# Moving four transpose pairs within the gate matmuls of an S5-plus-SwiGLU kernel with one PSUM slot for them

## The chip, the cores and the metric

The kernel runs on one core of one Trainium2 chip. The metric is the device time of one execution in microseconds (us), the median over several runs. A profile of one execution of each kernel goes with it. PE is the engine of the matmuls, PEld its weight loads, DVE is VectorE, ACT is ScalarE, POOL is GpSimd, and SP issues most DMAs. The later runs were made on three chips (numbers 0, 2 and 9 in the record), so times are compared only with those of before in the same rounds on the same chip, unless the text says otherwise.

## The reference, cut to what matters

```python
x  = A_x                                  # 1 x 2048 x 512, bfloat16
xn = layernorm(x)
return x + S5(xn, Lambda, B, C, dt, Dskip) \
         + (silu(xn @ w_gate) * (xn @ w_up)) @ w_down      # 512 -> 1376 -> 512
```

S5 is a diagonal complex recurrence over the 2048 tokens, between two matrix products of 512 x 512. All matmuls want `xn` with features on the partitions, so `xn` has to be transposed. The change touches only the first 512 tokens (four tiles of 128). Their transposes run on PE, through PSUM. The other tokens are transposed by DMA.

## The kernel before: the parts that matter

The kernel is written as a graph of tasks. PE and SP run their tasks in the order of the program. The orders of the other engines come from a list scheduler that works with estimated times. Semaphore waits are derived from what each task reads and writes. A task that reads or writes PSUM names whole banks:

```python
def BK(b):
    return [("bk", b, 0), ("bk", b, 1)]
...
for t in stream:                      # emission of one engine's stream
    for sem, val in t.waits:
        eng_obj.wait_ge(sem, val)     # t.waits: list of a dict that was filled
    inst = t.fn(eng_obj)              # in the order of a Python set
```

The first stage computes seven of the gate's column tiles for the first 512 tokens. It goes by quarters `q` of 128 tokens, so that it can start when the first tile of `x` is normalised. Seven of the eight PSUM banks accumulate these seven tiles. One bank is left, and all transposes of tiles 1 to 3 go through it (`xt_pair[0]`, here called the slot). A tile's 512 features are transposed in two halves of two 128x128 transposes each. After each half an engine copies the slot to SBUF.

```python
def xt_tile_fine(a, h, slot=None):            # tile a, half h
    slot = xt_pair[0] if slot is None else slot
    def tr2(e):
        for j in range(2):
            inst = e.transpose(out=ptr[:, slot, j*128:(j+1)*128], in_=xn_sb[...], identity=ident[:])   # cut; L582
        return inst
    g.add("pe", tr2, reads=[("xh", a, h), ("ident",)], writes=BK(slot), ...)
    if a == 3:     # VectorE copies the half, L589
    elif h == 0:   # ScalarE copies it in two pieces of 128 columns, L592
    else:          # ScalarE copies it in one piece of 256 columns, L597
...
place = {(0, 2, 4): (1, 0), (1, 0, 3): (1, 1), (1, 2, 2): (2, 0), (2, 0, 4): (2, 1), (2, 2, 2): (3, 0), (3, 0, 2): (3, 1)}
for q in range(4):
    for k0, k1 in (((0,1),(1,2),(2,3),(3,4)), ((0,1),(1,2),(2,4)), ((0,1),(1,2),(2,4)), ((0,2),(2,4)))[q]:
        for n, (i, bk) in enumerate(tiles):           # seven gate tiles
            if (q, k0, n) in place:
                xt_tile_fine(*place[(q, k0, n)])
            # matmuls kt = k0 .. k1-1 of gate tile i, tokens of quarter q          (L803)
            # reads xnT of tile q, features kt
ffn_mm(0, NQ, "g", xt_pair[0])       # the eighth gate tile, whole: 128x512 matmuls, L759
```

A quarter is 28 matmuls of 128x128. `place` says in front of which of them a transpose pair stands. So the second half of tile 1 (`(1, 1)`) has three things to wait for: VectorE's normalised operand, ScalarE's copy of the first half out of the slot, and PE's own order. The matmuls of quarter 1 with `kt` 2 and 3 then wait for the copy of that second half.

Of the kernel before, what the change touches and what calls it, by code (L numbers as in the profile page):

```python
# [249 lines left out]
def bass_parallel_sum__ssm_conv_s5__swiglu_ffn__prompt_kernel(  # L250
# [32 lines left out]
    with es:  # L283
# [87 lines left out]
        def next_pair():  # L371
            for _ in range(NB // 2):
                b = 2 * (pair_ctr[0] % (NB // 2))
                pair_ctr[0] += 1
                if not (b in reserved or _bank_live(b) or _bank_live(b + 1)):
                    return b
            raise AssertionError("all PSUM pairs live")
# [4 lines left out]
        def BK(b):  # L382
            return [("bk", b, 0), ("bk", b, 1)]
# [81 lines left out]
        def act_table(func, order):  # L465
            g.add("act", lambda e: e.activation(out=sm[:, NSM - 1, 0:1], in_=epst[:], func=func, bias=epst[:, 0:1]), reads=[("epst",)], writes=[("sm", "_warm")],
                  name="act_warm", est=1500, order=order)
# [3 lines left out]
        def pe_warm(n, w=512, bk=None):  # L471
            if bk is None:
                bk = next_pair()

            def mm(e, bk=bk):
                for _ in range(n):
                    inst = e.matmul(pbank[:, bk, 0:w], lhsT=one.to_broadcast([128, 128]), rhs=one.to_broadcast([128, w]), start=True, stop=True)
                return inst
            g.add("pe", mm, writes=BK(bk), name="pe_warm", est=n * w * 0.84, ninst=n)
# [96 lines left out]
        def xt_tile_fine(a, h, slot=None):  # L576
# [4 lines that stand above are left out]
                    kt = h * 2 + j  # L581
                    inst = e.transpose(out=ptr[:, slot, j * 128:(j + 1) * 128],  # L582
                                       in_=xn_sb[:, a % NXN, kt * 128:(kt + 1) * 128], identity=ident[:])
                return inst
            g.add("pe", tr2, reads=[("xh", a, h), ("ident",)], writes=BK(slot), name="xT%d_%d" % (a, h), est=2 * 64, ninst=2)
            dst, src = xnT[:, 0, a % 4, 2 * h:2 * h + 2, :], ptr[:, slot, 0:256].rearrange("p (k t) -> p k t", k=2)
            wr = [("xnTq", a, 2 * h + j) for j in range(2)] + ([("xnT", 0, a % 4)] if h else [])
            if a == 3:
                t = g.add("dve", lambda e: e.tensor_copy(out=dst, in_=src), reads=BK(slot), writes=wr, name="xTev%d_%d" % (a, h), est=320, order=(hold["xn3"],))  # L589
            elif h == 0:  # L590
                for j in range(2):
                    t = g.add("act", lambda e, j=j: e.activation(out=dst[:, j], in_=src[:, j], func=AF.Identity), reads=BK(slot), writes=wr[j:j + 1],  # L592
                              name="xTev%d_0%d" % (a, j), est=240, order=(t,) if j else ())
                    if j == 0:
                        hold["ev%da" % a] = t
            else:
                t = g.add("act", lambda e: e.activation(out=dst, in_=src, func=AF.Identity), reads=BK(slot), writes=wr, name="xTev%d_%d" % (a, h), est=340)  # L597
            hold["ev%d%d" % (a, h)] = t
# [154 lines left out]
        def ffn_mm(c, i, which, bk):  # L753
            fs = fsz[i]
            w = wg if which == "g" else wu

            def mm(e, bk=bk, w=w, i=i, fs=fs, c=c):
                for kt in range(KT):
                    inst = e.matmul(pbank[0:fs, bk, :].rearrange("p (j t) -> p j t", j=4), lhsT=w[:, kt, i * 128:i * 128 + fs], rhs=xnT[:, c % 2, :, kt, :],  # L759
                                    start=(kt == 0), stop=(kt == KT - 1))  # L760
                return inst
            g.add("pe", mm, reads=wres("wg" if which == "g" else "wu", i) + [("xnT", c % 2, j) for j in range(4)],
                  writes=BK(bk), name="mm_%s%d_%d" % (which, c, i), est=4 * 216, ninst=4)

        def silu_pair(c, ip, bk):
            i0, n = FP[ip]
            rows = slice(0, 128)
            sl = gctr[0] % NG
            gctr[0] += 1
            sg_slot[(c, ip)] = sl  # L770
            g.add("act", lambda e: e.activation(out=sg[rows, sl, 0:n, :].rearrange("p a t -> p (a t)"), in_=pair_f32(rows, bk, 512 * n), func=AF.Silu),  # L771
                  reads=sum([BK(bk + k) for k in range(n)], []), writes=[("sg", sl)], name="silu%d_%d" % (c, ip), est=63 + 427 * n)
# [8 lines left out]
        def ffn_gate_quarters(pairs):  # L781
            banks = {ip: next_pair() for ip in pairs}
            reserved.update(banks.values())
            tiles = [(2 * ip + k, banks[ip] + k) for ip in pairs for k in range(2)]
            xt_pair[0] = tiles.pop()[1]
            wbank = tiles[-1][1]
            pe_warm(9, 512, wbank)
            pe_warm(2, 128, wbank)
            ln_chunk0()
            xt_tile_fine(0, 0, wbank)  # L790
            pe_warm(1, 256, tiles[-2][1])
            xt_tile_fine(0, 1)
            pe_warm(1, 256, tiles[-2][1])
            place = {(0, 2, 4): (1, 0), (1, 0, 3): (1, 1), (1, 2, 2): (2, 0), (2, 0, 4): (2, 1), (2, 2, 2): (3, 0), (3, 0, 2): (3, 1)}
            for q in range(4):
                for k0, k1 in (((0, 1), (1, 2), (2, 3), (3, 4)), ((0, 1), (1, 2), (2, 4)), ((0, 1), (1, 2), (2, 4)), ((0, 2), (2, 4)))[q]:
                    for n, (i, bk) in enumerate(tiles):
                        if (q, k0, n) in place:
                            xt_tile_fine(*place[(q, k0, n)])

                        def mm(e, bk=bk, i=i, q=q, k0=k0, k1=k1):
                            for kt in range(k0, k1):
                                inst = e.matmul(pbank[:, bk, q * 128:(q + 1) * 128], lhsT=wg[:, kt, i * 128:(i + 1) * 128], rhs=xnT[:, 0, q, kt, :],  # L803
                                                start=(kt == 0), stop=(kt == KT - 1))
                            return inst
                        g.add("pe", mm, reads=[("wg", "a%d" % max(k - 1, 0)) for k in range(k0, k1)] + [("xnTq", q, k) for k in range(k0, k1)], writes=BK(bk),
                              name="mm_gq%d_%d_%d" % (i, q, k0), est=(k1 - k0) * 56, ninst=k1 - k0)
            reserved.clear()
            seq = ["sd0", "negm0", "nmr0", "xa01", "ev0a", "ev00", "sd1", "ev01", "ev1a", "ev10", "sd2", "ev11", "ev2a", "ev20", "sd3", "ev21"]
            for a_, b_ in zip(seq, seq[1:]):  # L810
                hold[b_].od.add(hold[a_])
            act_table(AF.Silu, (hold["ev21"],))
            hold["evac"] = g.tasks[-1]
            ffn_mm(0, NQ, "g", xt_pair[0])
            for ip in pairs:
                silu_pair(0, ip, banks[ip])
            hold["evac"] = [t for t in g.tasks if t.name == "silu0_0"][0]
# [124 lines left out]
        def dc_chunk(c, mid=None, split_last=False):  # L942
# [22 lines left out]
            for (lt, c0, nc_), bk in zip(items, banks):  # L965
# [13 lines left out]
                if nc_ == 128 and c0 == 256:  # L979
# [3 lines left out]
                    reads=[("xo", a, c) for c in ((256, 384) if nc_ == 128 else (c0,))], out_=True)  # L983

        ffn_gate_quarters([0, 1, 2, 3])
        params_a()
        tables()
# [103 lines left out]
```

## Time and profile before

| | before |
|---|---|
| time, first three runs | 179.34 us median (179.16 to 179.64) |
| span of the profiled run | 177.4 us |
| PE busy, VectorE busy | 98%, 92% |
| gate stage (first 128x128 gate matmul to first 128x512 one) | 5.770 to 12.826 us: 7.056 us |
| steps between matmuls over 56 ns in that stage | 134 ns in sum |

Part 1 and part 4 of the page of before: each engine's busy time with its share of the span, and the chain of work that ended last.

```profile
PE 173.6 (98%) x927; PEld 83.8 (47%) x935; DVE 162.5 (92%) x284; ACT 88.1 (50%) x116; POOL 9.0 (5%) x22
...
PE 95%; DMA 1%; DVE 1%; ACT 1%; issue 0%
```

The list of what PE waited for, in before (engine, line, releaser: total us, times, longest):

```profile
PE pb L477 <- PEq L1076: 0.8, 1, 0.8
PE pb L582 <- ACT xn_sb L548: 0.2, 1, 0.2
```

Both waits lie ahead of the gate stage. PE is nearly the whole chain. So the time is the start-up, plus PE's own work, plus whatever PE waits in the gate stage. The list does not show those last waits: they are tens of nanoseconds long and hidden in the overlap of pipelined matmuls. One has to look at starts. PE's timeline of before (start us, us, engine, line, operation, count), with L582 a transpose pair and L803 the gate matmuls between:

```profile
6.77 0.28 PE L582 MATMUL pb<-ident,xn_sb 128*128 128x128 bf16 x2
6.88 0.89 PE L803 MATMUL pb<-xnT,wg 128*128 128x128 bf16 x13
7.61 0.28 PE L582 MATMUL pb<-ident,xn_sb 128*128 128x128 bf16 x2
7.72 1.04 PE L803 MATMUL pb<-xnT,wg 128*128 128x128 bf16 x15
8.60 0.28 PE L582 MATMUL pb<-ident,xn_sb 128*128 128x128 bf16 x2
8.71 0.94 PE L803 MATMUL pb<-xnT,wg 128*128 128x128 bf16 x14
9.50 0.27 PE L582 MATMUL pb<-ident,xn_sb 128*128 128x128 bf16 x2
9.61 1.03 PE L803 MATMUL pb<-xnT,wg 128*128 128x128 bf16 x14
10.48 0.28 PE L582 MATMUL pb<-ident,xn_sb 128*128 128x128 bf16 x2
...
12.83 0.38 PE L759 MATMUL pb<-xnT,wg 128*128 128x512 bf16 x1
```

Read it as start to next start over the count. The 13 matmuls from 6.88 to 7.61 take 0.73 us, 56 ns each, so nothing waits there. The 15 from 7.72 to 8.60 take 0.88 us where 15 x 56 ns are 0.84, so about 40 ns are lost. The 14 from 9.61 to 10.48 take 0.87 us where 0.78 are due, so about 90 ns are lost. The single matmuls of the trace give the exact steps: 25 + 11 ns extra at 8.36 us, 8 ns at 9.50, 80 + 10 ns at 10.25. In this document "excess" is the sum of what such steps take over 56 ns.

Why PE waits at 8.36 and 10.25 us, and why the second transposes stand where they stand, is in ScalarE's timeline and in that of the weight loads, both of before. L592 copies a first half, L597 a second half:

```profile
7.08 0.45 ACT L592 ACTIVATE xnT<-pb 128x128 bf16<-128x128 bf16 x2 [0.70 <-PE pb L582]
...
7.92 0.38 ACT L597 ACTIVATE xnT<-pb 128x256 bf16<-128x256 bf16 x1
8.91 0.45 ACT L592 ACTIVATE xnT<-pb 128x128 bf16<-128x128 bf16 x2 [0.60 <-PE pb L582]
```

```profile
7.58 0.13 PEld L582 LDWEIGHTS pb<-ident,xn_sb 128*128 128x128 bf16 x2
...
9.47 0.13 PEld L582 LDWEIGHTS pb<-ident,xn_sb 128*128 128x128 bf16 x2
```

The copy of tile 1's first half ends at 7.53 us, and the weight load of its second transpose starts at 7.58. The copy of tile 2's first half ends at 9.35 us (8.91 + 0.45, to 0.01), and the weight load of its second transpose starts at 9.47.

### The profile page before, as it was taken

Reading aid. Unit: us, or ns where it says so; the run is one execution under the profiler, and the core shown is the slowest. Engines: PE = TensorE matmul, PEld = TensorE weight load, DVE = VectorE, ACT = ScalarE, POOL = GpSimd, SP = SyncE. Lnnn points to the kernel's source line nnn. Section 1 sums busy time; section 2 is a strip of 40 time slices with the busy share of each in tenths; the row PEclk is TensorE's granted clock in tenths of the full one; section 3 lists DMA queues with packets and bytes.
Section 4 is the critical chain, followed back from the end, with each engine's and each line's share of the span. In section 5 each row is a group of like instructions: output and inputs, shape, how many; then the busy total and the mean of one; then the engine's idle time right before and its main releaser. Section 6 shows DMA issues by size and latency. Waiting matters only on the chain.

```text
span 177.4 us, 2421 instructions
## 1 busy us (share of the span) xinstructions
PE 173.6 (98%) x927; PEld 83.8 (47%) x935; DVE 162.5 (92%) x284; ACT 88.1 (50%) x116; POOL 9.0 (5%) x22
## 2 busy tenths in 40 slices
PE   8999999999999999999999999999999999999994
PEld 2894444444444444444444444444444444444743
DVE  2956999799999999999999999999899999999933
ACT  4679989689999665044565560000965520000000
POOL 3023200040000000300000000000000000000000
PEclk9999999999999999999999999999999999999999
DMA  5994662664951000002600000002000000001022
GB/s 165 315 371 115 139 124 59 163 136 115 351 107 20 0 0 0 0 30 77 133 3 0 0 0 4 0 30 83 5 0 4 0 0 0 0 0 52 11 89 89
DMA packets 23014, 12.37 MB, mean 70 GB/s; under 512 B 15228, under 2 KB 23004, under 8 KB 23004
## 3 DMA queue, kind: packets, MB, share of 16 engines
q1 hardware_dynamic: 22508, 11.54, 23.9%
q10 hardware_dynamic: 496, 0.69, 1.1%
q8 instruction: 7, 0.11, 0.2%
q14 instruction: 3, 0.02, 0.0%
HBM read 6.46 MB, written 2.10 MB: 48 GB/s over the span
## 4 chain that ended last, share of the span: by engine, by line
PE 95%; DMA 1%; DVE 1%; ACT 1%; issue 0%
PE pb L759 36%; PE pb L959 21%; PE pb L876 16%; PE pb L972 15%; PE pb L803 4%; PE pb L839 2%; DMA x_sb<-in_A_x_dram 1%; PE pb L849 1%; PE pb L582 1%; DVE st L530 0%; ACT xn_sb L548 0%; ACT nm L545 0%; ACT sd L524 0%; DVE x_sb L977 0%; DVE mv L522 0%
## 5 line engine op out<-in xcount | busy, mean ns | idle before, releaser
L916 DVE TENSOR_TENSOR_SCAN rot<-sm,car,rot 128x512 bf16<-128x512 f32 x32 | 38.9, 1266 | 0.1
L959 PE MATMUL pb<-wd,hT 128*128 128x512 bf16 (+3 forms) x194 | 38.1, 355 | 0.2
L759 PE MATMUL pb<-xnT,wu 128*128 128x512 bf16 x160 | 37.3, 379 | 0.0
L759 PE MATMUL pb<-xnT,wg 128*128 128x512 bf16 x132 | 31.3, 379 | 0.0
L972 PE MATMUL pb<-W,hss 128*128 128x512 bf16 (+2 forms) x140 | 28.1, 355 | 0.2
L876 PE MATMUL pb<-xnT,BT 128*128 128x512 bf16 x128 | 28.1, 379 | 0.0
L959 PEld LDWEIGHTS pb<-wd,hT 128*128 128x128 bf16 (+1 forms) x198 | 18.5, 98 | 19.9
L759 PEld LDWEIGHTS pb<-xnT,wu 128*128 128x128 bf16 x160 | 15.6, 98 | 18.9 <-issue 0.2
L771 ACT ACTIVATE sg<-pb 128x1024 bf16<-128x1024 f32 x20 | 20.2, 1025 | 8.6 <-PE pb L759 7.8
L829 ACT ACTIVATE uf<-pb 128x1024 bf16<-128x1024 f32 x20 | 20.6, 1029 | 7.2 <-PE pb L759 6.1
L972 PEld LDWEIGHTS pb<-W,hss 128*128 128x128 bf16 x144 | 13.5, 98 | 14.3
L759 PEld LDWEIGHTS pb<-xnT,wg 128*128 128x128 bf16 x132 | 12.7, 98 | 15.7 <-issue 0.4
L876 PEld LDWEIGHTS pb<-xnT,BT 128*128 128x128 bf16 x128 | 12.5, 98 | 15.1
L883 ACT ACTIVATE u_sb<-pb 128x1024 bf16<-128x1024 f32 x16 | 16.2, 1018 | 5.6 <-PE pb L876 5.4
L977 DVE TENSOR_TENSOR x_sb<-pb,x_sb 128x512 bf16<-128x512 f32 (+2 forms) x18 | 11.0, 622 | 3.5 <-PE pb L972 3.4
L831 DVE TENSOR_TENSOR hT<-sg,uf 128x1024 bf16<-128x1024 bf16 x20 | 13.3, 679 | 0.0
L506 ACT ACTIVATE xn_sb<-x_sb,nmr,rstd 128x512 bf16<-128x512 bf16 x8 | 6.0, 803 | 9.2 <-DVE nmr L503 9.2
L858 ACT ACTIVATE sg<-pb 96x1024 bf16<-96x1024 f32 x2 | 2.0, 1014 | 17.1 <-PE pb L839 17.1
L482 DVE BATCH_NORM_STATS2 st<-x_sb 128x6 f32<-128x512 bf16 x12 | 7.4, 678 | 2.9 <-DMA x_sb<-in_A_x_dram 2.9
L907 DVE TENSOR_TENSOR rot<-rot,cosT 128x2048 bf16<-128x2048 bf16 x8 | 9.7, 1216 | 0.1
L907 DVE TENSOR_TENSOR rot<-rot,sin 128x2048 bf16<-128x2048 bf16 x8 | 9.7, 1217 | 0.0
L907 DVE TENSOR_TENSOR rot<-u_sb,cosT 128x2048 bf16<-128x2048 bf16 x8 | 9.7, 1215 | 0.0
(81 smaller groups left out, 143.3 us busy)
## 6 DMA issues: line engine op xcount, KB each, us to landing
out_dram<-x_sb SPq DMA_DIRECT2D x15, 128.0 KB, 1.7
x_sb<-in_A_x_dram SPq DMA_DIRECT2D x3, 512.0 KB, 7.0
wd<-in_B_w_down_dram SPq DMA_DIRECT2D x1, 1280.0 KB, 6.4
wu<-in_B_w_up_dram SPq DMA_DIRECT2D x1, 768.0 KB, 5.1
wu<-in_B_w_up_dram SPq DMA_DIRECT2D x1, 608.0 KB, 7.2
x_sb<-in_A_x_dram SPq DMA_DIRECT2D x4, 128.0 KB, 3.3
wg<-in_B_w_gate_dram SPq DMA_DIRECT2D x1, 480.0 KB, 6.0
wg<-in_B_w_gate_dram ACTq DMA_DIRECT2D x1, 448.0 KB, 3.8
```

What stands on the lines that cost most here:

```text
L482: return g.add("dve", lambda e, a=a: e.bn_stats(out=st[:, a, :], in_=x_sb[:, a, :]), reads=[("x", a)], writes=[("st", a)], name="bnst%d" % ...
L759: inst = e.matmul(pbank[0:fs, bk, :].rearrange("p (j t) -> p j t", j=4), lhsT=w[:, kt, i * 128:i * 128 + fs], rhs=xnT[:, c % 2, :, kt, :], ...
L771: g.add("act", lambda e: e.activation(out=sg[rows, sl, 0:n, :].rearrange("p a t -> p (a t)"), in_=pair_f32(rows, bk, 512 * n), func=AF.Sil ...
L829: g.add("act", lambda e: e.activation(out=uf[rows, ul, 0:n, :].rearrange("p a t -> p (a t)"), in_=pair_f32(rows, bk, 512 * n), func=AF.Ide ...
L831: g.add("dve", lambda e: e.tensor_tensor(out=hT[rows, hb, i0:i0 + n, :], in0=sg[rows, sl, 0:n, :], in1=uf[rows, ul, 0:n, :], op=ALU.mult), ...
L876: inst = e.matmul(pbank[:, bk, :].rearrange("p (j t) -> p j t", j=4), lhsT=BT[:, ri, kt, pt * 128:(pt + 1) * 128], rhs=xnT[:, c % 2, :, kt ...
L883: g.add("act", lambda e: e.activation(out=u_sb[:, us].rearrange("p r t -> p (r t)"), in_=pair_f32(slice(0, 128), b0), func=AF.Identity), r ...
L907: tt = lambda out, a, b, op, r, w, nm: g.add("dve", lambda e: e.tensor_tensor(out=out, in0=a, in1=b, op=op), reads=r, writes=w, name="%s_% ...
L916: g.add("dve", lambda e, A0=A0, A1=A1, k=k, ri=ri, pt=pt: e.tensor_tensor_scan(out=A1[:, k, ri, :], data0=rr[:, pt:pt + 1].to_broadcast([1 ...
L959: inst = e.matmul(pbank[:, bk, 0:nc_], lhsT=hT[0:fs, hb, i, lt * 128:(lt + 1) * 128], rhs=wd[0:fs, i, c0:c0 + nc_], start=(i == 0), stop=F ...
L972: inst = e.matmul(pbank[:, bk, 0:nc_], lhsT=hss[:, hb, pt, ri, lt * 128:(lt + 1) * 128], rhs=W12[:, ri, pt, c0:c0 + nc_], start=False, sto ...
L977: g.add("dve", lambda e, bk=bk, a=a, c0=c0, nc_=nc_: e.tensor_tensor(out=x_sb[:, a, c0:c0 + nc_], in0=pbank[:, bk, 0:nc_], in1=x_sb[:, a, ...
```

## The change

The intent is plain from the excess at 8.36 and 10.25 us. The transposes whose results come late go sooner in PE's order: tile 1's second half by one gate matmul, tile 2's second half by two, both halves of tile 3 by one place of two matmuls. Nothing is added or removed.

```diff
-            place = {(0, 2, 4): (1, 0), (1, 0, 3): (1, 1), (1, 2, 2): (2, 0), (2, 0, 4): (2, 1), (2, 2, 2): (3, 0), (3, 0, 2): (3, 1)}
+            place = {(0, 2, 4): (1, 0), (1, 0, 2): (1, 1), (1, 2, 2): (2, 0), (2, 0, 2): (2, 1), (2, 2, 1): (3, 0), (3, 0, 1): (3, 1)}
```

## The prediction

> **What bounds the kernel.** The page gives a span of 177.4 us with PE busy for 98%; in the chain of waits PE holds 95%. The list of PE's waits has two: 0.8 us at the start, 0.2 us at 5.52 us. From 12.83 us on no matmul waits for VectorE or ScalarE; the gaps left are steps of some 216 ns extra at changes of operand. VectorE is busy for 92%, but its last result that PE needs (hss) ends at 165.25 us, 4.6 us before its use at 169.89. So only a change of PE's time at the end of the gate stage (5.77 to 12.83 us) counts, one for one.
>
> **What the change does.** No instruction is added or removed. Tile 1's second transpose pair moves up by one gate matmul, tile 2's second by two, both of tile 3 by one place of two matmuls. A 128x128 matmul steps 55 to 56 ns start to start in the trace (as the Trainium skill, "TensorE: Matmul & The Clock Gate", section "Wait — 56ns, not 53.3ns?", states), so the moves are 56, 112, 112 and 112 ns.
>
> **What there is to win.** Matmul starts in the timeline show only these longer steps: 81 and 67 ns at 8.36 us (waiting for ScalarE's copy of tile 1's second half, 7.92 to 8.31), 64 ns at 9.50, 136 and 66 ns at 10.25 (copy of tile 2's second half, 9.81 to 10.19). The excess sums to 0.134 us, 0.07% of 179.34: the ceiling.
>
> **What takes it back.** These transposes share one PSUM slot, so a second half may start only after ScalarE has copied the first half out. Tile 1: that copy ends at 7.530 and the second half's weight load starts at 7.580, 24 ns behind its normal step: already bound by the copy, though the pipeline hides it. Tile 2: the copy ends at 9.353, a semaphore instruction on PE runs 9.390 to 9.441, weight load 9.466, matmul 8 ns late. Neither can start noticeably sooner; PE will wait in front of the transpose instead of behind it. Estimates from these times: tile 1 gets about 40 ns of new stall and loses the 36 ns at 8.36; tile 2 gets about 100 ns (40 if PE's two semaphore waits are emitted in the other order) and loses the 90 ns at 10.25. Net -0.06 to +0.03 us. Tile 3's halves really go 0.11 us sooner (slot free, operands ready at 10.18 and 10.44), so VectorE's copies and the parameter work move up about 0.1 us, but no PE wait hangs on them.
>
> **Prediction.** 179.34 us becomes 179.33 us; 178.95 to 179.75 in 8 of 10 cases, mostly the spread between runs (179.16 to 179.64). Faster by over 2%: 0.005; within 2%: 0.99; slower by over 2%: 0.005.
>
> **What would show it.** In PE's timeline the excess near 8.36 and 10.25 us is gone, and stands just before the second transposes of tiles 1 and 2, whose starts (7.61, 9.50) stay within 30 ns (tile 2: up to 90 ns sooner in the other wait order); VectorE's copies of tile 3 start near 10.68 and 11.57 instead of 10.79 and 11.68; the first 128x512 gate matmul at 12.83 plus or minus 0.06 us; PE's work after it unchanged.
>
> **What would make it wrong.** VectorE's and ScalarE's orders come from a list scheduler fed with estimated times; moving PE tasks may reshuffle them later and put waits on PE. Or the start-up of a run differs.

## The result, and the profile after

| | before | after |
|---|---|---|
| time, six runs each | 179.47 us median (179.16 to 179.74) | 179.32 us median (179.26 to 179.45) |
| ratio of after to before | | 0.9993, 95% interval 0.998 to 1.0006 |
| span of the profiled run | 177.41 us | 177.52 us |
| first gate matmul | 5.770 us | 5.826 us |
| gate stage | 7.056 us | 7.117 us |
| from there to the end | 164.583 us | 164.581 us |

Six runs of each kernel cannot tell the two times apart. Ratios in this document are the mean time of one kernel's fast runs over that of the other's fast runs of the same rounds, so they are not quite the ratios of the medians quoted.

The page and PE's waits of after:

```profile
PE 173.5 (98%) x935; PEld 83.7 (47%) x935; DVE 162.7 (92%) x284; ACT 88.0 (50%) x116; POOL 11.7 (7%) x22
...
PE 96%; DMA 1%; DVE 1%; ACT 1%; issue 0%
```

```profile
PE pb L477 <- PEq L1076: 0.8, 1, 0.8
PE pb L582 <- DVE xn_sb L517: 0.6, 1, 0.6
PE pb L582 <- ACT xn_sb L548: 0.2, 1, 0.2
```

The new 0.6 us line ends at 5.00 us, before the gate stage. PE's warm-up matmuls were done earlier in this run (3.54 us long instead of 4.12), so PE stood idle until tile 0 was normalised. It costs nothing: those matmuls have no result that anything uses. POOL's 2.7 us more in the page are nearly all in two of its lines (L490 and L494, six operations in each trace); the profile's spans on POOL are rough, and PE's list names no wait for POOL.

PE's timeline of after, the same stretch:

```profile
6.86 0.28 PE L582 MATMUL pb<-ident,xn_sb 128*128 128x128 bf16 x2
6.98 0.83 PE L803 MATMUL pb<-xnT,wg 128*128 128x128 bf16 x12
7.68 0.28 PE L582 MATMUL pb<-ident,xn_sb 128*128 128x128 bf16 x2
7.80 1.06 PE L803 MATMUL pb<-xnT,wg 128*128 128x128 bf16 x16
8.70 0.28 PE L582 MATMUL pb<-ident,xn_sb 128*128 128x128 bf16 x2
8.81 0.83 PE L803 MATMUL pb<-xnT,wg 128*128 128x128 bf16 x12
9.60 0.27 PE L582 MATMUL pb<-ident,xn_sb 128*128 128x128 bf16 x2
9.71 0.94 PE L803 MATMUL pb<-xnT,wg 128*128 128x128 bf16 x14
10.49 0.28 PE L582 MATMUL pb<-ident,xn_sb 128*128 128x128 bf16 x2
...
12.94 0.38 PE L759 MATMUL pb<-xnT,wg 128*128 128x512 bf16 x1
```

Do the same division. The 16 matmuls from 7.80 take 0.90 us, 56 ns each: nothing is lost at tile 1's consumers now. The 14 from 9.71 take 0.78 us: nothing at tile 2's either. But the 12 in front of tile 1's second transpose take 0.70 us instead of 0.67, and the 12 in front of tile 2's take 0.79 instead of 0.67. The waits have moved from behind the second transposes to in front of them. From the single matmuls: 31 + 10 ns in front of tile 1's, 119 ns in front of tile 2's, 160 ns in all, against 134 before. Another 40 ns of excess stand in front of tile 1's first transpose, which the change does not move. In this run tile 2's `x` came late: VectorE's first statistics of that tile started 0.10 us after the first gate matmul, in before 0.07 us ahead of it. VectorE's normalised tile 1 was late with it. Without those 40 ns the stage is about 0.02 us longer than before.

ScalarE's copies and the weight loads of the second transposes of after:

```profile
7.18 0.45 ACT L592 ACTIVATE xnT<-pb 128x128 bf16<-128x128 bf16 x2 [0.74 <-PE pb L582]
...
9.01 0.45 ACT L592 ACTIVATE xnT<-pb 128x128 bf16<-128x128 bf16 x2 [0.62 <-PE pb L582]
```

```profile
7.68 0.11 PEld L582 LDWEIGHTS pb<-ident,xn_sb 128*128 128x128 bf16 x2
...
9.57 0.13 PEld L582 LDWEIGHTS pb<-ident,xn_sb 128*128 128x128 bf16 x2
```

From the end of the copy to the weight load it is again 0.05 us for tile 1 (7.63 to 7.68) and 0.11 us for tile 2 (9.45 to 9.57), although PE was there sooner. From a tile's first transpose pair to its second it is 0.823 us for tile 1 (0.837 before) and 0.901 us for tile 2 (0.902 before).

### The profile page after: what moved, and what is told of

Same layout as the page of the kernel before. It is cut to its first block, busy times and chain, and to the rows that moved or that the text cites. A ratio compares the mean times of both kernels' runs of the same rounds, so it can differ in the third digit from the quotient of the medians.

```text
span 177.5 us, 2429 instructions
## 1 busy us (share of the span) xinstructions
PE 173.5 (98%) x935; PEld 83.7 (47%) x935; DVE 162.7 (92%) x284; ACT 88.0 (50%) x116; POOL 11.7 (7%) x22
## 4 chain that ended last, share of the span: by engine, by line
PE 96%; DMA 1%; DVE 1%; ACT 1%; issue 0%
PE pb L759 36%; PE pb L959 21%; PE pb L972 16%; PE pb L876 16%; PE pb L803 4%; PE pb L839 2%; DMA x_sb<-in_A_x_dram 1%; PE pb L849 1%; PE pb L582 1%; DVE st L530 0%; ACT xn_sb L548 0%; ACT nm L545 0%; ACT sd L524 0%; DVE x_sb L977 0%; DVE mv L522 0%
## 5 line engine op out<-in xcount | busy, mean ns | idle before, releaser
L959 PE MATMUL pb<-wd,hT 128*128 128x512 bf16 (+3 forms) x198 | 38.8, 355 | 0.0
```

The source lines that it names most:

```text
L959: inst = e.matmul(pbank[:, bk, 0:nc_], lhsT=hT[0:fs, hb, i, lt * 128:(lt + 1) * 128], rhs=wd[0:fs, i, c0:c0 + nc_], start=(i == 0), stop=F ...
```

## The experiments

My theory: the second transposes of tiles 1 and 2 are bound by the one PSUM slot, that is, by ScalarE's copy of the first half, so moving them up moves PE's wait from behind them to in front of them. The part of tile 3 is real, but no PE wait hangs on it. Rivals: the spread between runs hides a real gain of up to 0.13 us; the second transposes wait for their operands from VectorE; or VectorE, 92% busy, is binding too.

A gain of 0.1 us cannot be seen in a time whose runs spread over 0.3 us and more. So most experiments either make an effect several times larger, or are read in the matmul starts of their own trace. The list scheduler would reshuffle VectorE and ScalarE when PE's tasks change. So in every experiment their orders and GpSimd's are fixed to those of the kernel after, and only what the diff shows differs. The order of the two waits in front of the second transposes of tiles 1 and 2 is fixed as well, because in the original it varies from build to build (three builds of before gave two orders). The diffs are against the kernel after unless the text says otherwise, shorten the lines, and leave this fixing out:

```diff
-                t.waits = list(waits.values())
+                t.waits = _pinned(t, list(waits.values()), eng_sems)     # order of the two waits, per tile
...
-        streams = _schedule(g.tasks, engs)
+        streams = _frozen(_schedule(g.tasks, engs))                      # ACT, DVE, POOL as in after
```

All twelve runs gave correct results. The eleven runs of before in the rounds of r_after, f_far, d_pe and d_dve range from 179.12 to 180.63 us. The one of 180.63 has no trace and is in the ratios; without it the ratios of r_after, f_far and d_pe would be 1.0013, 1.0033 and 1.0054 instead of 1.0007, 1.0026 and 1.0047. The table comes first, then the runs one by one. "Slot" is the excess in front of the second transposes plus the excess at their consumers. "Start-up" is the excess that the change does not touch (matmuls at the slow clock, late loads). "Rest" is from the first 128x512 matmul to the end of the span.

| run | distance tile 1, tile 2 (us) | slot, tile 1 + tile 2 (ns) | start-up (ns) | gate stage (us) | rest (us) | time, median (us) |
|---|---|---|---|---|---|---|
| before | 0.837, 0.902 | 36 + 98 | 0 | 7.056 | 164.583 | 179.47 |
| after | 0.823, 0.901 | 41 + 119 | 40 | 7.117 | 164.581 | 179.32 |
| r_after | 0.902, 0.813 | 120 + 42 | 250 | 7.333 | 164.583 | 179.62 |
| f_far | 0.913, 0.813 | 399 + 376 | 77 | 7.769 | 164.587 | 179.96 |
| d_pe | 0.901, 0.813 | 119 + 40 | 0 | 8.169, pads in it | 164.583 | 180.36 |
| d_dve | 0.913, 0.813 | 121 + 41 | 542 | 7.621 | 165.861 | 179.62 |
| d_dve2 | 0.902, 0.812 | 120 + 40 | 0 | 7.077 | 164.650 | 179.55 |
| w2_fused | 0.822, 0.813 | 40 + 41 | 223 | 7.226 | 164.596 | 179.29 |
| b_best | 0.845, 0.838 | 35 + 35 | 7 | 6.999 | 164.576 | 179.20 |
| s2_one | 0.813, 0.812 | 320 + 375 | 416 | 8.036 | 165.446 | 181.14 (one) |
| s2_two | 0.502, 0.447 | 0 + 0 | 0 | 6.920 | 165.448 | 179.94 (one) |
| p2_tile1 | 0.812, 0.901 | 40 + 98 | 0 | 7.060 | 164.578 | 179.26 (one) |
| p2_tile2 | 0.837, 0.902 | 35 + 121 | 0 | 7.079 | 164.581 | 179.35 (one) |
| p2_tile3 | 0.837, 0.902 | 36 + 99 | 0 | 7.057 | 164.570 | 179.35 (one) |

s2_two has no excess at all. Its 124 matmuls (112 gate matmuls and 12 transposes) took 6.920 us, 55.8 ns each. The Trainium skill states the same step for a warm array ("TensorE: Matmul & The Clock Gate", section "Wait — 56ns, not 53.3ns?"). Every other gate stage in the table, apart from d_pe's pads, is this 6.920 us plus its excess, to within 0.01 us.

### r_after: the kernel after again

The place is that of after. The two waits were to be fixed as in the first trace.

> The kernel after, built again, with the order of its other engines and of the two semaphore waits before the second transposes of tiles 1 and 2 fixed as they were in its first trace. Theory (the transposes are bound by the PSUM slot, gain and loss cancel): ratio to before 1.000 within 0.0015; from the start of a tile's first transpose pair to that of its second 0.82 us for tile 1 and 0.90 us for tile 2, as in both first traces; matmul steps longer than 56 ns stand in front of those second pairs (excess about 40 and 119 ns) and nowhere at the consumers. Rival (the change is a real gain of 0.13 us that the spread hid): ratio 0.9993 or lower again, and no excess in front.

Measured: 179.62 us (179.47 to 179.81, 5 runs), ratio to before 1.0007, 95% interval 0.998 to 1.0034; before was 179.45 us in the same rounds. The sum of the slot's excess was 162 ns, as in after (160). But the tiles had changed roles: 0.902 us and 120 ns for tile 1, 0.813 us and 42 ns for tile 2. My fixing had worked the other way round. The compiled program carries the first wait of the list on the transpose, and the second becomes a semaphore instruction of its own ahead of it. That accident is evidence: the excess followed the order of the waits and not the tile. The first traces say the same once one looks. In after, tile 2's semaphore instruction starts at 9.490 us, 28 ns after the semaphore of ScalarE's copy at 9.462, and ends at 9.541; the weight load follows at 9.566. For tile 1 the semaphore is at 7.634 us and the weight load at 7.677; the separate instruction there, VectorE's, was over at 7.558.

The other finding of this run is its start-up: 250 ns more in the gate stage. The first five steps between its gate matmuls took 104 to 107 ns instead of 56, until 6.50 us. PE was still at half speed, although it had been busy since 0.83 us. The Trainium skill has this: TensorE starts at half clock and gets the full one after a while of activity, counted in windows that do not start with the kernel ("TensorE: Matmul & The Clock Gate", section "What's actually happening"). The section "Wait — 56ns, not 53.3ns?" of the same page gives 106.7 ns as the slow step, and this trace agrees. The granted clock of the profile says 1.0 all the same. So one start-up can cost nearly twice the ceiling of this change. The expected distances failed, because the fixing was reversed, and the sum of the slot's excess came as expected.

### f_far: five and six matmuls sooner still

```diff
-   ... (1, 0, 2): (1, 1), ... (2, 0, 2): (2, 1), ...
+   ... (0, 3, 4): (1, 1), ... (1, 2, 5): (2, 1), ...
```

> As after, but the second transposes of tile 1 and tile 2 stand five and six gate matmuls sooner still (279 and 335 ns of matmul steps). Slot theory: the distance from first to second transpose pair stays 0.82 and 0.90 us (within 0.03), PE waits some 0.3 and 0.45 us in front of them, the gate stage (first 128x128 gate matmul to first 128x512 one, 7.06 us before, 7.12 after) becomes about 7.7 us, and the time rises by about 0.6 us, ratio to before 1.003 to 1.004. Rival (the operands, not the slot, or nothing holds them): the distances shrink to 0.54 and 0.57 us, the gate stage stays at 7.0 to 7.1 us and the ratio is 1.000.

Measured: 179.96 us (179.86 to 180.08, 5 runs), ratio 1.0026, 95% interval 1.0002 to 1.005. PE's timeline of f_far, tile 1's pairs and then tile 2's:

```profile
6.93 0.29 PE L582 MATMUL pb<-ident,xn_sb 128*128 128x128 bf16 x2
7.06 0.55 PE L803 MATMUL pb<-xnT,wg 128*128 128x128 bf16 x7
7.85 0.27 PE L582 MATMUL pb<-ident,xn_sb 128*128 128x128 bf16 x2 [0.24 <-DVE mv L522]
...
9.13 0.28 PE L582 MATMUL pb<-ident,xn_sb 128*128 128x128 bf16 x2
9.24 0.50 PE L803 MATMUL pb<-xnT,wg 128*128 128x128 bf16 x6
9.94 0.28 PE L582 MATMUL pb<-ident,xn_sb 128*128 128x128 bf16 x2 [0.20 <-ACT xnT L592]
```

With 7 and 6 matmuls between instead of 12 and 12, the second transposes still came 0.91 and 0.81 us after the first. They had not become sooner by anything; PE waited 399 and 376 ns. For tile 2 the profile names the releaser: ScalarE's copy of the first half, L592. For tile 1 it names a VectorE statistic that no transpose reads. Here the late wait sits on the separate semaphore instruction, and the profile puts the wait down to what came last by its clock. The slot's excess grew by 613 ns over r_after (775 against 162), as expected. The ratio of 1.0026 lies below the expected 1.003 to 1.004, though the interval holds them. The time grew by less than the expected 0.6 us, by 0.34 us of medians over r_after and 0.5 us over before, because r_after started worse: in the profiled runs the spans differ by 0.33 us, which is the 0.61 us of the slot, less r_after's 0.25 us of slow clock and its 0.11 us later first gate matmul, plus f_far's 0.08 us of late `x`. The rival (no binding, distances of 0.50 and 0.45 us) is out. I had written 0.54 and 0.57 for it, a slip in counting; s2_two measures them.

### s2_one and s2_two: a second PSUM bank

The rival that the operands hold the second transposes is tested by giving them another bank. A column range of the same bank would not do. The Trainium skill ("PSUM — Partial Sum Buffer", section "PSUM bank collisions raise a hardware error") says that PE writing a bank while ScalarE reads it in the same partitions raises an error even at disjoint columns; no run here shows that. So the seventh gate tile leaves the stage. Its matmuls are replaced by matmuls with zero weights into the sixth tile's bank, which add nothing, and it is computed whole afterwards (4 x 216 ns more). Both kernels do this, with f_far's places. Only s2_two uses the freed bank. Against f_far, with both of ScalarE's waits riding on the transposes:

```diff
+        zer = sb("zer", [128, 128], B16)                           # zeroed by GpSimd
...
+                        bk = tiles[min(n, 5)][1]
-                                ... lhsT=wg[:, kt, i * 128:(i + 1) * 128], ...
+                                ... lhsT=zer[:] if n == 6 else wg[:, kt, i * 128:(i + 1) * 128], ...
...
+            ffn_mm(0, 6, "g", wbank)
             ffn_mm(0, NQ, "g", xt_pair[0])
# s2_two only:
-                            xt_tile_fine(*place[(q, k0, n)])
+                            xt_tile_fine(*place[(q, k0, n)], slot=wbank if place[(q, k0, n)][1] else None)
```

> Control for s2_two. The seventh gate tile's place in the stage is taken by matmuls with zero weights into the sixth tile's bank (result unchanged), and the seventh tile is computed whole afterwards, so a second PSUM bank is free; it is not used here. Places as in f_far, ScalarE's wait riding. Slot theory: distances 0.81 to 0.83 us, steps of some 0.3 and 0.37 us in front of the second transposes of tiles 1 and 2.

> As s2_one, with the second transposes in the second PSUM bank. Slot theory: nothing holds them, distances shrink to the bare matmul steps, 9 x 56 = 0.50 us for tile 1 and 8 x 56 = 0.45 us for tile 2, no long step in front, and none at the consumers; gate stage 6.92 us plus what the start-up adds (cold matmuls, late x of tile 2), some 0.6 us shorter than s2_one. Rival (operands from VectorE, or PE's own order, hold them): distances stay above 0.7 us.

Measured, in one look each: s2_one had distances of 0.813 and 0.812 us with 320 and 375 ns in front. s2_two had 0.502 and 0.447 us with no step over 56 ns anywhere in the stage. PE's timeline of s2_one, the second halves of tile 1 and tile 2 with the pairs before them:

```profile
7.35 0.28 PE L582 MATMUL pb<-ident,xn_sb 128*128 128x128 bf16 x2
...
8.16 0.28 PE L582 MATMUL pb<-ident,xn_sb 128*128 128x128 bf16 x2
...
9.46 0.28 PE L582 MATMUL pb<-ident,xn_sb 128*128 128x128 bf16 x2
...
10.27 0.28 PE L582 MATMUL pb<-ident,xn_sb 128*128 128x128 bf16 x2 [0.20 <-ACT xnT L592]
```

The same four pairs of s2_two:

```profile
6.84 0.27 PE L582 MATMUL pb<-ident,xn_sb 128*128 128x128 bf16 x2
...
7.34 0.28 PE L582 MATMUL pb<-ident,xn_sb 128*128 128x128 bf16 x2
...
8.63 0.28 PE L582 MATMUL pb<-ident,xn_sb 128*128 128x128 bf16 x2
...
9.08 0.28 PE L582 MATMUL pb<-ident,xn_sb 128*128 128x128 bf16 x2
```

That settles the mechanism: the slot held the transposes, and the operands did not. The gate stage was 6.920 us, as expected. s2_one's was 8.036, of which 0.42 us were matmuls at the slow clock; the remaining difference is 0.70 us, where some 0.6 were expected. The rest of both was 165.45 us, 0.865 us more than elsewhere, the four added matmuls. As a version for use s2_two is no gain: it pays 0.86 us in matmuls for at most 0.14 us of waiting.

### p2_tile1, p2_tile2, p2_tile3: one part at a time

These are before with one part of the change, the waits emitted as in the first traces.

```diff
# against before, one line each
-(1, 0, 3): (1, 1)      +(1, 0, 2): (1, 1)                               # p2_tile1
-(2, 0, 4): (2, 1)      +(2, 0, 2): (2, 1)                               # p2_tile2
-(2, 2, 2): (3, 0), (3, 0, 2): (3, 1)   +(2, 2, 1): (3, 0), (3, 0, 1): (3, 1)   # p2_tile3
```

> Before, with tile 1's move alone, waits emitted as in the first traces. Theory: 30+10 ns in front of tile 1's second transpose, nothing left at its consumer; tile 2 as before (8 in front, 90 at the consumer); sum 139 ns, before 134. Rival (the move is a gain): sum about 98.

> Before, with tile 2's move alone, waits as in the first traces (ScalarE's wait of tile 2 as the separate instruction). Theory: tile 1 as before (36 at the consumer); tile 2 119 ns in front, nothing at its consumer; sum 155 ns. Rival (the move is a gain): sum about 44.

> Before, with the two moves of tile 3 alone. Theory: excess as before, sum 134 ns; VectorE's copies of tile 3 0.11 us sooner, 4.91 and 5.80 us after the first gate matmul instead of 5.02 and 5.91; everything after the gate stage 164.58 us as in all runs. Rival (tile 3 is where the gain lies): stage shorter by 0.1 us or the rest shorter.

Measured: slot excess 138, 156 and 135 ns, where 139, 155 and 134 were expected and before has 134. So tile 1's part costs about 4 ns and tile 2's about 22 ns. Tile 3's part costs nothing and does what it was meant to: VectorE's copies start 4.913 and 5.806 us after the first gate matmul, in before 5.020 and 5.914. Nothing after it becomes faster: the rest is 164.570 us. The one time of each (179.26, 179.35, 179.35, beside one of before at 179.36) says no more than that nothing large happened.

### w2_fused: both of ScalarE's waits on the transposes

```diff
 # order of the waits of the second transposes of tiles 1 and 2
-(as in after: ScalarE's wait rides on tile 1's transpose, is a separate instruction for tile 2's)
+ScalarE's wait rides on both; VectorE's long fulfilled wait is the separate instruction
```

> As after, but for both second transposes the wait on ScalarE's copy rides on the transpose instruction itself and the (long fulfilled) wait on VectorE is the separate semaphore instruction. The runs so far had one tile each way and the excess in front went with it: 31+10 ns where ScalarE's wait rides, 119 ns where it is separate, on tile 1 as on tile 2. Theory (the separate semaphore instruction costs the difference): 30+10 ns in front of both, distances 0.82 and 0.81 us, gate stage 0.08 us shorter than after's for the same start-up, no measurable change of the time (ratio within 0.002 of 1.000). Rival (tile 1 or tile 2 is slow by its own copy): one distance stays 0.90.

Measured: 40 and 41 ns, distances 0.822 and 0.813 us. From the semaphore of ScalarE's copy to the weight load it is 42 ns for tile 1 when the wait rides (7.910 to 7.952 us). When it is separate it is 106 ns (r_after's tile 1: semaphore 7.992, semaphore instruction 8.021 to 8.072, weight load 8.098). Within the one trace of after it is 43 ns for tile 1, where it rides, and 104 ns for tile 2, where it does not. The Trainium skill says that an instruction waiting on several engines may get separate semaphore instructions ahead of it ("Perfetto Trace Analysis", section "Identifying Dependency Chains"). This trace agrees, and shows what the order costs: about 64 ns at the weight load, 80 to 90 ns at the matmul. The gate stage was 7.226 us, with 223 ns of late `x` in it. The time, 179.29 us (179.16 to 179.61), ratio 1.0001 (0.9988 to 1.0015), shows none of it, as expected.

### b_best: arriving when the slot comes free

```diff
-   ... (1, 0, 2): (1, 1), ... (2, 0, 2): (2, 1), ...
+   ... (1, 0, 3): (1, 1), ... (2, 0, 3): (2, 1), ...      # waits as in w2_fused
```

> As w2_fused, with tile 1's second transpose back at its place of before and tile 2's second transpose one matmul sooner than before, so that both arrive when the slot comes free. Theory: no step over 56 ns in front of either; at the consumers 36 ns for tile 1 as before and about 26 for tile 2; sum about 62 ns against 134 of before and 160 of after. Worth 0.07 us, so the time does not show it: ratio within 0.002 of 1.000. Rival (the excess merely moves, its sum is fixed): about 130 to 160 ns again.

Measured: nothing in front of the second transposes, 35 ns at each consumer, 70 in all where 62 were expected, against 134 before and 160 after. So the sum is not fixed. Most of the gain over after is the order of the waits and not the place: w2_fused, with the places of after, already has 81 ns, so the places of b_best are worth 11 ns more. The places of before with this order of the waits were not run. The gate stage was 6.999 us, the shortest of those that compute the whole of it. The time was 179.20 us (179.11 to 179.67, 5 runs), ratio 0.9999 (0.9983 to 1.0015), before 179.32 us in the same rounds. By the trace this beats both kernels by about 0.06 and 0.09 us; by the clock no difference can be told.

### d_pe: is PE's time worth its face value?

```diff
+            pe_warm(5, 512, xt_pair[0])          # five 128x512 matmuls into the free slot
             ffn_mm(0, NQ, "g", xt_pair[0])
```

> As after, with five 128x512 warm-up matmuls into the free PSUM slot at the end of the gate stage, all other orders fixed. Theory that a change of PE's time at the end of the gate stage counts one for one: 5 x 216 ns = 1.08 us more than after, ratio to before 1.006 (1.005 to 1.007). Rival (slack behind it, another engine ends the kernel): less than 0.5 us more, ratio below 1.003.

Measured: 180.36 us (180.27 to 180.47, 5 runs), ratio 1.0047, 95% interval 1.0024 to 1.0071. In the trace the pads take 1.09 us at the end of the gate stage, and the rest is 164.583 us as in before, so the trace shows a worth of one for one. The ratio came out below the expected 1.005 to 1.007, whose centre lies within the interval. Against r_after the medians differ by 0.74 us only. Between their profiled runs the spans differ by 0.65 us: 1.09 us of pads, less the 0.18 us by which r_after's first gate matmul came later and the 0.25 us that r_after lost to the slow clock. How the runs without a profile started is not known.

### d_dve, twice: does VectorE's time behind tile 3 matter?

```diff
+            for _ in range(2): g.add("dve", lambda e: e.memset(rot[:, 0, 0], 0.0), ...)   # after the copy of tile 3's second half
+            (all parameter work of VectorE ordered behind them)
```

> As after, with two memsets of a 128x2048 bf16 buffer on VectorE behind its copy of tile 3's second half, so that the parameter work starts some 1 to 2 us later, ten times and more what the change gives it. Theory (no PE wait hangs on VectorE's time there; its last result has 4.6 us to spare): ratio to before within 0.0015 of 1.000, the list of PE's waits unchanged. Rival (VectorE at 92% busy binds too): 1 to 2 us longer, ratio 1.005 or more.

> The same kernel as d_dve again, because the profiled run of d_dve was one of late loads (181.2 us; the other five 179.45 to 179.88), in which PE waited 1.1 us for the transposing load of the second B matrix. Theory: that was the loads, not VectorE; the parameter work starts some 2 us later than in after and the work behind the gate stage still takes 164.58 us, ratio to before within 0.002 of 1.000. Rival (the late VectorE makes PE wait): a PE wait again behind the gate stage, 165 us or more for it.

Measured, first time: 179.62 us median of 6 runs, equal to r_after, but the profiled run was one of 181.2 us. In it the loads came late: tile 2's `x` cost 442 ns in front of tile 1's first transpose, and the first part of `w_up` landed at 11.33 us, in the other traces at 9.8 to 10.6, all before the first memset began at 12.81. Later PE waited 1.1 us for the second transposed B matrix. The ratio to before, 1.0021, and its interval of 0.9988 to 1.0053 include that run. A run more than 1 us above its median is not peculiar to the memsets: before has one of 180.63 us in the same rounds, though no trace shows its cause.

Second time, the same kernel: 179.55 us (179.3 to 179.67, 6 runs), ratio 1.0006, 95% interval 0.9989 to 1.0023. VectorE's timeline of the second run: the copy of tile 3's second half, the second memset, and the first of the parameter work:

```profile
11.66 0.29 DVE L589 COPY xnT<-pb 128x256 bf16<-128x256 bf16 x1 [0.60 <-PE pb L582]
...
13.31 0.91 DVE L812 MEMSET rot<- 128x1024 uint32 x1 [0.28 <-DVE rot L812]
14.14 0.10 DVE L658 SCALAR_TENSOR_TENSOR sm<-sm,prT 128x4 f32<-128x4 f32 x1
```

In before this work (L658) starts at 11.89 us. It was 2.2 us later here, twenty times what the change could give. The list of PE's waits has the three entries of after, all ahead of the gate stage. The rest is 164.650 us, 0.07 us more than elsewhere: PE stepped 62 and 10 ns late at 25 us, where the second B matrix had landed at 25.02 us (at 22.99 in before, where PE wanted it at 24.91). In both runs with the memsets the two B matrices took 9.5 and 9.7 us from the landing of the `x` ahead of them, in the other twelve traces 8.1 to 8.7. Whether the late VectorE work slows those loads, or chance did it twice, no run here separates. So a share of d_dve's 1.1 us may be due to the memsets; that is not excluded. What the runs do show is that PE waited for no VectorE result behind the gate stage with the work 2.2 us late, and that the 0.1 us alone, in p2_tile3, left the rest at 164.570 us, in before 164.583.

## Why the prediction was right

The time was predicted as 179.33 us, within 178.95 to 179.75, and came out at 179.32 us. That the two agree to 0.01 us is luck: a drop of 0.01 us was predicted, the medians of six runs each differ by 0.15 us, and by the trace the stage became slightly longer. What can be judged is "no difference by the clock", which held, and the mechanism. Point by point:

- *Ceiling of 0.134 us, 0.07% of the time.* Right. s2_two, with no slot to wait for, takes 6.920 us for the stage where before takes 7.056 us, 0.136 us less.
- *The transposes are bound by the slot, so the wait goes from behind to in front.* Right, and shown: f_far (far sooner, distance unchanged) and s2_two (another bank, distance down to the bare matmul steps).
- *About 40 ns of new stall at tile 1, about 100 at tile 2, or 40 if PE's waits come in the other order.* Measured 41 and 119 in after, 41 at tile 2 in w2_fused. The size of 100 was low by 19 ns.
- *Net -0.06 to +0.03 us.* About +0.02 us. The parts add up: tile 1 about 4 ns, tile 2 about 22, tile 3 nothing.
- *Tile 3's halves go 0.11 us sooner, and nothing hangs on it.* Alone they do (p2_tile3: 0.107). In after the copies start only 0.046 us sooner by the stage's own clock, because PE's stage was itself about 0.06 us late by then. So "near 10.68 and 11.57" failed; they started at 10.80 and 11.69.
- *First 128x512 matmul at 12.83 plus or minus 0.06 us; second transposes within 30 ns of 7.61 and 9.50.* These failed as absolute times: 12.94, 7.68 and 9.60 us. The step that failed is that I took the start-up as equal in both runs. It began 0.056 us later and lost 0.040 us to a late load. Counted from each tile's first transpose, the second pairs moved by 14 and 1 ns.
- *"The gaps left are steps of some 216 ns extra at changes of operand".* This was a misreading. Before's trace has 927 matmul records where after's has 935, and the profile can lack a few. The chain of waits of before, from 65 us on:

```profile
65.07 9.46 PE pb L959 x43
74.53 1.30 PE pb L972 x6
75.83 0.05 issue
```

and of after:

```profile
65.13 9.51 PE pb L959 x44
74.65 5.40 PE pb L972 x25
```

The group has 44 matmuls; one record was missing in before, and its 216 ns looked like a gap. That it was no gap is shown by the rest, 164.583 us in before and 164.581 in after. Ten of the fourteen traces lack the same eight records. A gap of exactly one instruction's step should send one to the counts first. It did not hurt here, since the rest of the kernel was taken as unchanged.

- *VectorE has 4.6 us to spare, so PE waits on nobody behind the gate stage.* The conclusion held for VectorE, but 4.6 us was not the smallest margin behind the gate stage. The second B matrix, a load, lands 1.9 us before PE's use in before (22.99 against 24.91) and 0.7 us before it in p2_tile3 (24.39 against 25.13), and d_dve shows a run in which that load was what PE waited for.

## What to carry to other kernels

When a producer and its consumer are a few instructions apart on one engine and pass through a single buffer, look at what releases the buffer before moving the producer up: if that is already the last thing to arrive, moving it further up only moves the wait to the other side. The gain, if there is one, is in the buffer (another bank, s2_two), in what empties it (not tried here), or in how the wait is emitted: on PE, in these traces, it was cheaper to put the wait that is fulfilled last on the instruction itself and the early one on the separate semaphore instruction (40 against 120 ns of excess). And when the ceiling read from the trace is below the spread between runs, judge the change by distances within one trace, from a common event just ahead of it, because start and clock of the run shift everything else.

## What the Trainium skill lacked or had wrong

- "Perfetto Trace Analysis" says that separate semaphore instructions may be inserted for an instruction with several waits, but not what they cost or that their order counts: 106 ns from semaphore to weight load when the late wait is the separate one, 42 ns when it rides on the instruction.
- "TensorE: Matmul & The Clock Gate" gives the moment at which the array gets its full clock as about 4 us into sustained activity, plus or minus 500 ns, though it also says that the window runs free and that the number of slow matmuls varies. In the fourteen traces here, with PE busy from 0.83 us in all of them, the last matmul at the slow clock started anywhere from 2.91 to 6.67 us. In two of them gate matmuls ran at 104 to 107 ns steps and lost 0.25 and 0.42 us, more than the whole ceiling of the change. The step at the slow clock itself agrees with the page.
- "Perfetto Trace Analysis" does not warn that matmul records can be missing: before's trace lacks 8 of 935, each a false gap of 214 to 216 ns.
- No page that I read has the spread of load times within the start: between traces of kernels with the same first loads, VectorE's first statistics of tile 2 began from 0.17 us before the first gate matmul to 0.60 us after it, and cost PE up to 442 ns.
